# Block means of the first batch's values from single value tiles, two weights laid out contiguously, and a new order of the instructions

## The chip, the cores and the metric

One of the eight cores of a Trainium2 chip runs the kernel. The metric is device microseconds of one execution, as the median of three runs; the trace comes from one more execution, taken by the hardware profiler.

## The reference

Three layers follow each other on 2 batches of 768 tokens of 512 features.

1. Attention of 8 heads of 64. Each query sees a window of 31 keys around it and one summary per block of 32 tokens: the maximum of the block's keys, and the **mean of its values**.
2. Four experts, each a causal attention of width 64 over the 768 tokens. A gate keeps two of them for each token.
3. A channel mix: two blends of each token with the token before it, one through `relu(x @ w_k)**2 @ w_v`, one through `sigmoid(x @ w_r)`, and their product.

```python
k_sum = k.reshape(B, H, nb, block, D).max(axis=3)
v_sum = v.reshape(B, H, nb, block, D).mean(axis=3)
scores_s = scale * np.einsum('bhsd,bhnd->bhsn', q, k_sum) + np.log(block)
a = softmax(np.concatenate([masked(scores_l), scores_s], axis=-1))
x = np.matmul(a, np.concatenate([v, v_sum], axis=2))        # layer 1
...
out = sigmoid(xr @ w_r) * (np.maximum(xk @ w_k, 0.0) ** 2 @ w_v)   # layer 3
```

(The lines are shortened; `softmax` and `masked` stand for the reference's own lines.)

## The kernel before, in words

Layer 1 runs in tiles of 128 tokens, `t` = 0 to 11, six per batch. `stage1_scores` (from L554) makes a tile's scores on TensorE: for `t` below 3 straight from the key tensor `k0` and the key maxima `ksm[0]` (L589, L590), later from copies of its window, the slabs (`slab`, L459, and L584). `stage1_softmax` (L598) adds the mask and takes the maximum on VectorE (L607), takes the exponential on ScalarE (L610), sums and inverts (L613, L615), and scales by the result (L621, or L626 on ScalarE). `stage1_trans` transposes (L650), and `stage1_out` (L655) multiplies with the values (L668). Its operand holds the 96 value rows of a window and 24 rows of block means; `put_val_sums` (L531) copies the means there, on whichever engine the order names (L535 VectorE, L536 ScalarE, L538 GpSimd, L540 a DMA). A tile's result is split into a rounded part and the rest (`rnd`, L368, and `sub`, L376).

The means themselves are products with a constant matrix of 1/32 (`own`, L546): `val_sums` (L496) multiplies a value tile by it, four matmuls of 128 columns each, one per 128 features, into four bands of partitions of one PSUM bank `p`. For the first batch they take the six window tiles of `t` = 0 to 2, which lie two by two in SBUF (`vw`, each 128 rows with some that the next one shares), and one tile of three times 128 rows, `vt0`, loaded by one DMA of 768 KB. `val_sums_out` (L506) then copies the bands to SBUF, 24 x 128 each (L369 on ScalarE, L370 on VectorE). The two weights of the experts that the change touches, `wvg` and `wqk`, are loaded by `load_wvg` (L699) and `load_wqk` (L705), and split into the operands of L761 and L743.

Layer 2 is `proj_all` (L743 queries and keys, L761 values and gates) and `attention` (L843 scores, L903 transposes, L929 values, L971 output). Layer 3 is `rec` (L1123), `hid` (L1174: seven products for eight, with the sums of operands on VectorE or GpSimd at L1036 and L1037, evictions at L1147 and L1192) and `duo` (L1261, the same scheme for the second product). The 64-bit weights of layer 3 are unpacked on VectorE and ScalarE (L1012 to L1022).

The program does not run in the order in which it is written. Each step is recorded as an operation with what it reads and writes, with one or more `ways` (engines), and `Plan.run` (L268) issues them by the table `ORDER`: an entry divided by four is the number of the operation, the rest of the division the way. `HOMES` gives each buffer its slot. All DMAs are issued by SyncE (`load`, L359) in that order. An engine does its own instructions in this order, and waits for others by semaphores.

Of the kernel before, what the change touches and what calls it, by code (L numbers as in the profile page):

```python
# [16 lines left out]
B, H, S, D = 2, 8, 768, 64  # L17
DM = H * D
# [182 lines left out]
)  # L201

CUTS = (5, 9, 12)

EARLY = 3

FIRST = (0,)


class Buf:  # L210

# [104 lines left out]
def attn_moe_rwkv(  # L316
# [39 lines left out]
    def bank(name):  # L356
        return buf(name, [P, 512])
# [1106 lines left out]
```

## Time and profile before

| | us |
|---|---|
| median of three runs | 343.79 |
| lowest and highest of the three | 343.23, 344.01 |
| the profiled execution, its own time | 344.52 |
| its span in the trace | 342.7 |
| TensorE matmuls, busy | 325.3 |
| VectorE busy | 317.9 |
| ScalarE busy | 266.0 |
| GpSimd busy | 102.3 |

The profiled execution's time is 1.82 us more than its span, which is what lies around it, and 0.73 us more than the median of the runs. A busy share is a mean over stages: TensorE is busy in nearly all of the span, and VectorE too, so what an edit is worth is read from the short stretches in which TensorE waits, and from what it waits for there. TensorE's work stands twice in the trace, as weight loads (PEld) and as matmuls (PE); an fp32 matmul of the program shows as two records. The clock granted to TensorE is 1.00 in every stretch but that after the last matmul.

### The profile page before, as it was taken

What the parts mean: (1) busy time and instruction counts of PE and PEld (TensorE: products, weight loads), DVE (VectorE), ACT (ScalarE), POOL (GpSimd) and SP (SyncE); (2) the same over time, 40 slices, a digit from 0 to 9 for tenths busy, and PEclk for the clock granted to TensorE, in tenths of its full rate; (3) what the DMA queues carried; (4) which work ended last, traced back from release to release, by engine and by line L of the source; (5) the groups of instructions that cost most, each with busy time, mean ns of one, the idle gap of its engine ahead of it and who ended that gap; (6) DMA issues with size and microseconds to landing.
All of it is one profiled execution on the core that took longest, in us unless ns stands there. A gap on an engine that the chain in (4) does not pass through costs nothing.

```text
span 342.7 us, 8312 instructions
## 1 busy us (share of the span) xinstructions
PE 325.3 (95%) x3024; PEld 295.0 (86%) x3024; DVE 317.9 (93%) x930; ACT 266.0 (78%) x719; POOL 102.3 (30%) x112
## 2 busy tenths in 40 slices
PE   0899979999999999999999999999999999999995
PEld 0779969988889979789676899999999889999995
DVE  1889988999998898999999999999999999999995
ACT  1699989999898667668688789678996998787630
POOL 0556520514321154141530002125540200414550
PEclk9999999999999999999999999999999999999999
DMA  7999885585061000101142010101004000011223
GB/s 253 348 342 319 281 305 194 166 256 149 2 193 63 2 2 0 63 1 64 61 122 62 9 56 1 61 2 61 2 0 123 3 0 2 0 63 46 80 77 109
DMA packets 20160, 33.80 MB, mean 99 GB/s; under 512 B 2088, under 2 KB 9000, under 8 KB 20120
## 3 DMA queue, kind: packets, MB, share of 16 engines
q1 hardware_dynamic: 20120, 33.28, 29.7%
q8 instruction: 24, 0.39, 0.5%
q14 instruction: 16, 0.13, 0.1%
HBM read 29.63 MB, written 3.15 MB: 96 GB/s over the span
## 4 chain that ended last, share of the span: by engine, by line
PE 82%; DVE 13%; DMA 2%; issue 2%; SPq 1%; ACT 0%; DVEq 0%
PE ps L1261 17%; PE ps L1174 14%; PE ps L743 9%; PE ps L1123 6%; PE ps L761 5%; PE ps L843 5%; PE ps L903 5%; PE ps L929 5%; PE ps L668 4%; PE ps L971 4%; PE ps L650 3%; DVE b L377 3%; DVE t L1100 2%; PE ps L584 2%; DMA ks<-in_kS 2%
## 5 line engine op out<-in xcount | busy, mean ns | idle before, releaser
L1261 PE MATMUL ps<-w,s 128*128 128x256 f32 x336 | 48.9, 281 | 0.0
L1261 PEld LDWEIGHTS ps<-w,s 128*128 128x128 f32 x336 | 43.9, 188 | 0.1
L1174 PE MATMUL ps<-b,w 128*128 128x384 f32 x216 | 41.2, 338 | 0.4 <-DVE b L1192 0.4
L1174 PEld LDWEIGHTS ps<-b,w 128*128 128x128 f32 x216 | 38.1, 188 | 1.0 <-DVE b L1192 0.7
L743 PE MATMUL ps<-b,w 128*128 128x384 f32 x192 | 38.6, 345 | 0.0
L1123 PE MATMUL ps<-w,b 128*128 128x512 f32 x144 | 36.2, 397 | 0.0
L369 ACT ACTIVATE t<-ps 128x384 f32<-128x384 f32 (+1 forms) x59 | 25.9, 468 | 11.2 <-PE ps L903 6.2
L743 PEld LDWEIGHTS ps<-b,w 128*128 128x128 f32 x192 | 32.6, 188 | 0.7 <-issue 0.2
L369 ACT ACTIVATE b<-ps 128x384 f32<-128x384 f32 (+4 forms) x49 | 23.6, 492 | 9.6 <-PE ps L668 2.8
L1123 PEld LDWEIGHTS ps<-w,b 128*128 128x128 f32 x144 | 26.5, 188 | 5.3 <-issue 0.2
L610 ACT ACTIVATE w<-w,nm 128x120 f32<-128x120 f32 x72 | 27.8, 393 | 0.9 <-DVE nm L607 0.7
L369 ACT ACTIVATE b<-t 128x384 fp32r<-128x384 f32 x42 | 20.5, 517 | 6.6 <-DVE t L1100 4.0
L971 PE MATMUL ps<-u,w 128*128 128x384 f32 x96 | 22.0, 352 | 0.6 <-DVE u L377 0.6
L379 POOL TENSOR_TENSOR w<-s,w 128x512 fp32r<-128x512 f32 x13 | 17.8, 1379 | 14.5 <-ACT w L369 12.9
L377 DVE TENSOR_TENSOR b<-t,b 128x384 fp32r<-128x384 f32 x36 | 21.1, 602 | 0.0
L761 PE MATMUL ps<-q,b 128*128 128x260 f32 x144 | 20.9, 291 | 0.0
L1100 DVE SCALAR_TENSOR_TENSOR t<-b,mu,t 128x384 f32<-128x384 f32 x32 | 20.6, 661 | 0.1
L843 PE MATMUL ps<-ks,b 64*128 64x384 f32 (+3 forms) x192 | 20.0, 337 | 0.6 <-DVE t L370 0.6
L929 PE MATMUL ps<-t,b 128*64 128x384 f32 (+2 forms) x144 | 20.6, 421 | 0.0
L1037 POOL TENSOR_TENSOR t<-t,t 128x384 f32<-128x384 f32 (+1 forms) x4 | 5.1, 1286 | 46.8 <-ACT w L369 32.3
L761 PEld LDWEIGHTS ps<-q,b 128*128 128x128 f32 x144 | 18.6, 189 | 0.4 <-issue 0.2
L369 ACT ACTIVATE s<-u 128x512 fp32r<-128x512 f32 x24 | 14.5, 626 | 5.4 <-DVE u L1036 2.3
(204 smaller groups left out, 928.8 us busy)
## 6 DMA issues: line engine op xcount, KB each, us to landing
s<-in_wk SPq DMA_DIRECT2D x8, 512.0 KB
s<-in_wv SPq DMA_DIRECT2D x8, 512.0 KB, 4.1
w<-in_qT SPq DMA_DIRECT2D x12, 256.0 KB, 4.7
out_y<-t SPq DMA_DIRECT2D x24, 128.0 KB, 1.7
w<-in_vp SPq DMA_DIRECT2D x10, 256.0 KB, 4.2
s<-in_wr SPq DMA_DIRECT2D x4, 512.0 KB, 4.6
s<-in_kS SPq DMA_DIRECT2D x6, 320.0 KB
ks<-in_kS SPq DMA_DIRECT2D x4, 400.0 KB
```

Source lines behind the costliest of these rows:

```text
L369: ways = [("act", act(n, sb), lambda: nc.scalar.activation(dst(), src(), AF.Copy)), ("dve", dve2(n) if sb else dve(n), lambda: nc.vector.t ...
L377: ways = [("dve", dve(n), lambda: nc.vector.tensor_tensor(dst(), a(), b().bitcast(F32), ALU.subtract), sb)]
L610: op("act", act(NK, True) + 186, lambda i=i, z=z, pr=pr, nm=nm: nc.scalar.activation(pr()[:, i], pr()[:, i], AF.Exp, bias=nm.t[:, i:i + 1] ...
L743: mm(p.t[:, :C], a[kc].t[:, cols], x.t[:, kc, :], start=(kc == 0 and i == 0), stop=(kc == KC - 1 and i == 2))
L761: mm(p.t[:, :260], x.t[:, kc, tok], a[kc].t, start=(kc == 0 and i == 0), stop=(kc == KC - 1 and i == 2))
L843: mm(ps[e2].t[:, :z - a], q1.t[r, x, tok], ks.t[r, y, a:z], start=n == 0, stop=n == 2)
L929: mm(acc.t[64 * e2:64 * e2 + 64, tq0 * P:(tq0 + cnt) * P], vv.t[:, kb, e * D:(e + 1) * D], th[e2].t[:, i0 * P:(i0 + cnt) * P], start=first ...
L971: mm(p.t[:, :C], a[ep].t[:, m * P:(m + 1) * P], x.t[:, ep, :], start=(ep == 0 and i == 0), stop=(ep == 1 and i == 2))
L1100: op("dve", dve(C) + 60, lambda: nc.vector.scalar_tensor_tensor(tmp(), cur(), mu.t[:, i:i + 1], tmp(), ALU.mult, ALU.add), r=rd, w=[(mb, m ...
L1123: mm(p.t, a.t[:, kc, tok], w[2](), start=(kc == 0 and i == 0), stop=(kc == KC - 1 and i == 2))
L1174: mm(p.t[:, :C], a[2]()[:, o:o + P], x.t[:, u, j], start=not (j or i), stop=j == 1 and i == 2)
L1261: mm(p.t[:, :256], x.t[:, u, j * P:(j + 1) * P], v[2]()[:, col:col + 256], start=not (j or i), stop=j == FC // 2 - 1 and i == 2)
```

## The change

Four things change.

- The means of the first batch use the two window tiles of `t` = 0 alone (`PLAIN = 1`), and five tiles of 128 rows, each in a buffer of its own in the pool `w`, loaded by a DMA of 256 KB. Before they used six window tiles and three tiles in one buffer. So 7 groups of four matmuls are left of 9, and five DMAs stand for one.
- Their results go to two PSUM banks in turn (`p[g % 2]`); ScalarE copies those of one, VectorE those of the other where the order says so.
- `wvg` and `wqk` lie in memory with the rows of a partition together: a partition's 4160 or 4096 bytes are one piece, before four of 1040 or two of 2048.
- `ORDER` and `HOMES` are new throughout. Two planner costs of DMAs (the argument of `load`) changed with them; they have no effect on the program but by the order.

```diff
+PLAIN = 1
...
-        load(tf[0], src, P * S * 4, 360.0 if b else 300.0, w=[(tb, i)])
+        load(tf[0], src, P * (S if b else SPV) * 4, w=[(tb, i)])
...
-                    mm(p.t[32 * g:32 * g + NB, 0:P], own(j, s2), v()[:, g * P:(g + 1) * P],
+                    mm(p[g % 2].t[32 * g:32 * g + NB, 0:P], own(j, s2), v()[:, g * P:(g + 1) * P],
                        start=first and n == 0, stop=last and n == len(tiles) - 1)
...
-                lambda g=g: p.t[32 * g:32 * g + NB, 0:P], P, [p], [(vs, g)])
+                lambda g=g: p[g % 2].t[32 * g:32 * g + NB, 0:P], P, [p[g % 2]], [(vs, g)])
...
-        load(lambda: raw.t, wvg.rearrange("(k p) n -> p k n", p=P), P * 4160, w=[raw])
+        load(lambda: raw.t, wvg, P * 4160, w=[raw])
...
-    vt0 = val_tiles(0, "b6", EARLY, TPB)
+    vt0 = [val_tiles(0, "w", j, j + 1) for j in range(PLAIN, TPB)]
...
-    p = bank("ps")
-    for t in range(EARLY):
+    p = [bank("ps"), bank("ps")]
+    for t in range(PLAIN):
         for s2 in range(2):
             v = vw[t][s2]
             val_sums(v, p, [(t, s2, lambda v=v: v.t)], t + s2 == 0)
-    val_sums(*vt0[:1], p, vt0[1], last=True)
+    for v, tiles in vt0:
+        val_sums(v, p, tiles, last=v is vt0[-1][0])
...
 ORDER = (
-    12, 0, 52, 36, 16, 44, 24, 32, 76, 64, 80, 40, 56, 20, 172, 220, 72, 48, 228, 194, 28, 68, 60, 190, 232, 84,
...
```

Line numbers in the rows of the change are two to four higher than those of the kernel before, for the same code.

**SyncE, the first loads.** `qT` are queries, `kS` keys, `masks` the masks, `vp` values. Before:

```order
L360 DMA w_63<-in_qT 128x512
L360 DMA w_67<-in_qT 128x512
L360 DMA ks_69<-in_kS 128x800 x4
L360 DMA msk_74<-in_masks 128x120
L360 DMA w_76<-in_vp 128x512
```

With the change:

```order
L362 DMA w_65<-in_qT 128x512
L362 DMA ks_67<-in_kS 128x800 x4
L362 DMA msk_72<-in_masks 128x120
L362 DMA w_74<-in_qT 128x512
L362 DMA msk_72<-in_masks 128x240
```

The queries of the second tile (256 KB) stood ahead of the keys and now stand behind them.

**ScalarE, its first instructions**, with the semaphores that they wait for (DMAHW1 to DMAHW4 are the four loads of keys in the change). Before:

```order
L610 ACT_TABLE_LOAD
L610 ACTIVATE b_56_90,sms_65<-b_56_90,nm_91 128x120 [waits DVE_49]
```

With the change:

```order
L371 ACT_TABLE_LOAD [waits DMAHW3_49,DMAHW4_49,DMAHW2_49]
L371 ACTIVATE s_18_120<-ks_67 128x4x160 [waits DMAHW1_49]
L612 ACTIVATE b_60_88,sms_63<-b_60_88,nm_90 128x120 [waits DVE_49]
```

One of the three slab copies of 128 x 640 that GpSimd made now leads ScalarE's order, and the load of the function table stands behind the waits of that copy.

**TensorE around the means** (`ps_290` and `ps_291` are the banks of the means, `b_56`, `b_60` the first tile's weights). Before:

```order
L501 MATMUL ps_290<-w_125,cst_127 24x128 x4
L650 MATMUL ps_303<-cst_127,b_56_90 120x128
L501 MATMUL ps_290<-w_101,cst_127 24x128 x4
L501 MATMUL ps_290<-w_76,cst_127 24x128 x4
L501 MATMUL ps_290<-w_80,cst_127 24x128 x4
L501 MATMUL ps_290<-u_23_132,cst_127 24x128 x4
L650 MATMUL ps_303<-cst_127,b_56_90 120x128 x2
...
L501 MATMUL ps_290<-b_52_196,cst_127 24x128 x12
L650 MATMUL ps_377<-cst_127,b_67_151 120x128 x3
```

With the change:

```order
L503 MATMUL ps_290<-w_127,cst_125 24x128
L503 MATMUL ps_291<-w_127,cst_125 24x128
L652 MATMUL ps_318<-cst_125,b_60_88 120x128 x3
L652 MATMUL ps_327<-cst_125,b_60_88 120x128
...
L503 MATMUL ps_290<-w_201,cst_125 24x128
L503 MATMUL ps_291<-w_201,cst_125 24x128
L652 MATMUL ps_327<-cst_125,b_60_88 120x128
L652 MATMUL ps_364<-cst_125,b_72_154 120x128
```

Before, 4 matmuls of the means stood ahead of the first transpose, and 7 transposes and 16 matmuls of scores between the last of the means and the first use of them (L668). Now 12 of 28 stand ahead of the first transpose, and 10 transposes and 32 matmuls of scores between the last and the first use.

## Rows read from the trace of the kernel before

**Rows 1.** The page: span, and busy time by engine (us, share, instructions).

```profile
span 342.7 us, 8312 instructions
PE 325.3 (95%) x3024; PEld 295.0 (86%) x3024; DVE 317.9 (93%) x930; ACT 266.0 (78%) x719; POOL 102.3 (30%) x112
```

**Rows 2.** Stretch 10 to 20 us: length; busy PE, PEld, DVE, ACT, POOL; PEclk; DMA; GB/s.

```profile
10.00:20.00 10.00, 8.79 (x266) 7.22 (x262) 8.67 (x63) 8.49 (x45) 6.62 (x11) 1.00 1.01 353
```

**Rows 3.** Chain that ended last, in order of time: start us, us, what.

```profile
3.06 6.96 DMA ks<-in_kS
...
20.02 0.83 PE ps L501 x24
...
216.12 44.46 PE ps L1174 x252
...
279.36 59.69 PE ps L1261 x504
```

**Rows 4.** Timeline of SyncE's queue: start us, us, what is issued.

```profile
0.72 0.87 SPq L360 DMA_DIRECT2D w<-in_qT  x2
```

**Rows 5.** Timeline of ScalarE: start us, us, instruction [idle before it, releaser].

```profile
0.72 1.28 ACT L610 ACT_TABLE_LOAD   x1 [0.72 <-PEq L1453]
11.22 0.39 ACT L610 ACTIVATE b<-b,nm 128x120 f32<-128x120 f32 x1 [9.22 <-DVE nm L607]
...
20.87 1.11 ACT L369 ACTIVATE w<-ps 24x128 f32<-24x128 f32 x4 [0.33 <-PE ps L501]
```

**Rows 6.** Groups by form: line engine op shapes, count, busy us, mean ns, idle before.

```profile
L372 POOL TENSOR_SCALAR s<-ks 128x640 f32<-128x640 f32 x3 | 2.1, 727 | 9.3 <-DMA ks<-in_kS 9.3
L369 ACT ACTIVATE w<-s 128x512 fp32r<-128x512 f32 x19 | 11.8, 622 | 0.1
```

**Rows 7.** Timelines of GpSimd and of TensorE, first weights and first transpose.

```profile
15.02 1.93 POOL L621 TENSOR_TENSOR b<-b,rss 128x480 f32<-128x480 f32 x2 [1.77 <-DVE rss L615]
...
17.17 0.33 PE L650 MATMUL ps<-cst,b 128*120 128x128 f32 x1
```

**Rows 8.** Timelines of VectorE and of TensorE, the first use of the means.

```profile
22.02 1.17 DVE L535 COPY w<-w 24x512 f32<-24x512 f32 x2 [1.19 <-ACT w L369]
...
23.24 2.11 PE L668 MATMUL ps<-b,w 120*64 120x64 f32 x64 [0.54 <-DVE w L535]
```

**Rows 9.** What TensorE waited for: total us, times, longest us.

```profile
PE ps L668 <- issue: 1.8, 1, 1.8
PE ps L584 <- issue: 1.1, 1, 1.1
...
PE ps L1174 <- DVE b L1192: 0.4, 1, 0.4
```

**Rows 10.** Groups by form of VectorE, and four of a kind in its timeline.

```profile
L370 DVE COPY w<-ps 120x512 f32<-120x512 f32 x7 | 4.8, 685 | 0.1
L370 DVE COPY t<-ps 128x384 f32<-128x384 f32 x17 | 9.2, 548 | 1.6 <-PE ps L884 0.9 <-PE ps L903 0.5
L1100 DVE SCALAR_TENSOR_TENSOR t<-b,mu,t 128x384 f32<-128x384 f32 x32 | 20.6, 661 | 0.1
L377 DVE TENSOR_TENSOR w<-s,w 128x512 fp32r<-128x512 f32 x14 | 10.4, 740 | 0.0
...
204.18 1.96 DVE L377 TENSOR_TENSOR b<-t,b 128x384 fp32r<-128x384 f32 x4
```

**Rows 11.** Timelines of VectorE and GpSimd where both read SBUF.

```profile
212.05 1.39 DVE L1100 SCALAR_TENSOR_TENSOR t<-b,mu,t 128x384 f32<-128x384 f32 x1
...
211.81 1.21 POOL L1037 TENSOR_TENSOR t<-t,t 128x384 f32<-128x384 f32 x1 [32.29 <-ACT w L369]
...
314.31 7.45 POOL L379 TENSOR_TENSOR s<-u,s 128x512 fp32r<-128x512 f32 x1 [0.26 <-POOL t L1037]
```

**Rows 12.** DMA issues: out<-in, count, KB each, median us to landing.

```profile
w<-in_vp SPq DMA_DIRECT2D x10, 256.0 KB, 4.2
...
s<-in_wqk SPq DMA_DIRECT2D x2, 512.0 KB, 10.1
```

More of the change, by code (lines that the diff above doesn't have):

```diff
@@ L500, in go @@
                 for g in range(4):
-                    mm(p.t[32 * g:32 * g + NB, 0:P], own(j, s2), v()[:, g * P:(g + 1) * P],
+                    mm(p[g % 2].t[32 * g:32 * g + NB, 0:P], own(j, s2), v()[:, g * P:(g + 1) * P],
                        start=first and n == 0, stop=last and n == len(tiles) - 1)
-        op("pe", 230 * len(tiles), go, r=[vt, cst], w=[p], stream="p1v", mode="quarter")
+        op("pe", 230 * len(tiles), go, r=[vt, cst], w=p[:1] if p[0] is p[1] else p, stream="p1v", mode="quarter")
     def val_sums_out(b, p):
@@ L523, in sums1 @@
             key_sums(1, i, t, [lambda t=t: t.t] * 2, kS[1, :, i, HALO:HALO + S])
-        p = bank("ps")
+        p = [bank("ps")] * 2
         for j in range(0, TPB, 2):
@@ L707, in load_wqk @@
             raw = buf("s4", [P, 2, 512])
-            load(lambda raw=raw: raw.t, wqk[256 * k2:256 * k2 + 256].rearrange("(k p) n -> p k n", p=P), P * 4096,
+            load(lambda raw=raw: raw.t, wqk[:, 2 * k2:2 * k2 + 2], P * 4096,
                  w=[raw])
@@ L1353, in attn_moe_rwkv @@
     stage1(0, 1)
-    p = bank("ps")
-    for t in range(EARLY):
+    p = [bank("ps"), bank("ps")]
+    for t in range(PLAIN):
         for s2 in range(2):
@@ L1410, in _layout @@
     wk = moe_wk.reshape(2, 2, DM, D).transpose(2, 0, 1, 3).reshape(DM, 2, 1, P)
-    d["wqk"] = np.concatenate([wq, wk], axis=2).reshape(DM, 512)
-    d["wvg"] = np.concatenate([moe_wv.transpose(1, 0, 2).reshape(DM, E * D), moe_w_gate], axis=1)
+    d["wqk"] = np.concatenate([wq, wk], axis=2).reshape(KC, P, 512).transpose(1, 0, 2)
+    wvg = np.concatenate([moe_wv.transpose(1, 0, 2).reshape(DM, E * D), moe_w_gate], axis=1)
+    d["wvg"] = wvg.reshape(KC, P, E * D + E).transpose(1, 0, 2)
     d["wo"] = moe_wo.reshape(2, P, DM).transpose(1, 0, 2)
```

287 rows, old and new, of tables (HOMES, ORDER) are left out of this document.

## The prediction

> **What bounds the kernel now.** I read the busy shares first, then the chain that ended last, then what TensorE waited for, and last the timelines of the first 25 us. The shares [rows 1] show TensorE busy for 325.3 of 342.7 us and VectorE for 317.9: there is little idle time to win, 17.4 us on TensorE, and most of it lies ahead of the first keys and behind the last matmul. The chain [rows 3] says what holds each stretch. It begins with the loads of the keys, the last of which lands at 3.06 + 6.96 = 10.02 us. It then stays on TensorE nearly without a break, leaves it for VectorE for some thirty microseconds ahead of 216 us, and from 216.12 us on is TensorE up to the last few instructions: 252 records of L1174, and at last 504 of L1261, each without a wait. So the kernel is bound by TensorE behind a start that DMA sets, and a microsecond that is won early on TensorE is kept if VectorE, which has hardly more room, comes earlier too. TensorE's waits [rows 9] are few: 1.8 and 1.1 us for which the profile names no releaser ("issue"), and 0.4 us for VectorE at L1174; to these comes the wait of 0.54 us at 23.24 [rows 8], for the block means. These waits, the start, and the work itself are all that the change can shorten.
>
> **The change, part by part.**
>
> *The keys come earlier.* The queries of the second tile leave their place ahead of the keys. SyncE's queue spends 0.87 us on issuing two loads of queries [rows 4], so the keys are issued some 0.43 us earlier; and 262 kB less pass ahead of the last of them, at the 353 GB/s of the first full stretch [rows 2] 0.74 us. The bounds are 0.4 and 0.75 us, and I take 0.6: the transfers, not the issue, fill these microseconds, but the queue of the value loads behind the keys competes too.
>
> *ScalarE starts with a copy.* In the trace the function table is loaded at 0.72 us in 1.28 us, while nothing else could run, and the first exponential starts at 11.22 us [rows 5]. Now the table load waits for the keys, at about 10.02 - 0.6 = 9.4 us, and the slab copy follows. The copy of 128 x 640 was on GpSimd, 0.73 us; ScalarE takes 0.62 us for 128 x 512 [rows 6], by size 0.78 us for 640 columns. So ScalarE is free at 9.4 + 1.28 + 0.78 = 11.5 us, 0.25 us later than its first exponential before. The first tile's weights were scaled by GpSimd from 15.02 to 16.95 us, and the first transpose stood at 17.17 [rows 7]; both move 0.25 us late, to 17.2 and 17.4. TensorE, 0.6 us early, does not idle for that, since 8 more matmuls of the means now stand ahead of the first transpose: 16 records at 0.83 / 24 = 0.035 us [rows 3] are 0.55 us, and it arrives at 17.17 - 0.6 + 0.55 = 17.1. The 0.6 us are therefore spent on work that stood later; 0.1 to 0.3 us of waiting may be left, which lies within the bounds above. What covers ScalarE's late start is this reordering; without it 0.6 us would be lost again.
>
> *Fewer matmuls for the means.* 36 become 28, 8 fewer, or 16 records at 0.035 us: **0.55 us** less on TensorE, in a stretch where it is the chain.
>
> *The wait for the means.* Before, the last of them ended at 20.85 us, ScalarE copied four bands in 1.11 us [rows 5], VectorE copied the result behind it from 22.02 us, having waited 1.19 us, and TensorE started L668 at 23.24 us after a wait of 0.54 us [rows 8]. With two banks two engines copy two bands each, some 0.55 us in place of 1.11; and three transposes and 16 matmuls of scores more stand in between on TensorE. The wait of 23.24 - 20.85 = 2.4 us is then covered: **0.54 us** less, 0 at worst. VectorE's idle 1.19 us goes too, and so it keeps pace. Late next is the value weight `wvg`, whose parts are the operands of L761.
>
> *The loads.* Five loads of 256 KB replace one of 768 KB. A load of 256 KB lands 4.2 us after its issue [rows 12]. Up to the last value tile SyncE now issues some 0.5 MB less, since four window tiles move behind it, so none of the means waits for its tile. The `wqk` loads stand behind 0.26 MB more than before, 0.75 us at 353 GB/s; they landed 10.1 us after issue [rows 12], in a full queue, and their first user came later still. The contiguous weights move the same bytes in fewer pieces; the price of a piece stands in no row, and as no transfer but the keys is on the chain, I take 0 for it, between a loss of 0.75 us and a gain of as much.
>
> *The rest of the order.* Counted in the two orders, VectorE has 676 instructions ahead of its first L1192 in place of 682. What goes is above all four evictions of 120 x 512 (4 x 0.69), five of 128 x 384 (5 x 0.55) and two scalings of 128 x 480 (some 0.7 each, by size); what comes is three subtractions of 128 x 512 (3 x 0.74), three evictions of 24 x 128 and smaller ones (some 1.7 together). At these means of forms [rows 10] the difference is 6.9 - 3.9 = 3.0 us. Neighbours overlap: four L377 of 128 x 384 took 1.96 us, 0.49 apiece, where the mean of 128 x 512 gives 0.56 by size; so nearer 2.6 us. TensorE's wait there is only 0.4 us [rows 9], so I book **0.4 us** and leave the rest as room. The two waits without a releaser I leave where they are: the trace shows no cause, and the new order has the same instructions around the first.
>
> *GpSimd gets more.* It has 129 rows where it had 117. For that the trace has a warning: at 212.05 us one L1100 of VectorE took 1.39 us beside a GpSimd instruction that began at 211.81 [rows 11], where the mean of its form is 0.66 [rows 10]. Twelve more such pairs would be 12 x 0.73 = 8.8 us of VectorE; none costs nothing. I take 0, since VectorE's own work has become less, and since GpSimd was used as densely beside it before. The Trainium skill's page "SBUF — State Buffer", section "Who interferes with whom", says that a GpSimd instruction that reads SBUF and a VectorE instruction with two SBUF inputs share a port that one of them holds for its whole length, so that the other fully blocks. By that rule every added pair is at risk, and a sum with half of them would end 4.4 us higher than mine.
>
> The sum is 0.6 + 0.55 + 0.54 + 0.4 = 2.1 us. Against the profiled execution's own 344.52 us (span 342.7 and 1.82 around it) that gives 342.4; that execution lies 0.73 above the median of 343.79, so the median becomes **341.7 us**.
>
> **The rivals.**
>
> *Slower: GpSimd is starved in the last stage.* In `duo`, GpSimd had two instructions of 128 x 512 and now has five, sums that VectorE made before, and ScalarE and VectorE wait for their results in order. At 314.31 us such a subtraction took 7.45 us [rows 11], where VectorE never paused. The same page's rule agrees with that row. Each of the three new ones can be some 6 us late. TensorE stalls if its next operand is later than its lead; if half of the 6 us is covered, one such stall costs 3.0 us and gives 341.7 + 3.0 = 344.7. For it speaks that the chain of this stage is 504 records of TensorE without a break [rows 3], so that any wait is a loss; against it that the long one at 314.31 cost TensorE nothing. It decides as soon as one operand is late by more than the 2.1 us that were won.
>
> *No change.* The early microseconds are won, but the new order opens a wait elsewhere, or the unexplained waits [rows 9] come once more: 1.5 us, between 1.1 and 1.8, gives 343.2, and with the start's gain lost to ScalarE 343.8. For it speaks that VectorE is as full as TensorE, so that an order must hold both.
>
> *Much faster.* VectorE's 2.6 us less work closes the waits in the middle as well, and the start brings its full 0.75: some 2 us more, 339.7. Against it: TensorE's own work shrinks by 0.55 us alone, so this needs nearly every wait gone.
>
> **How the numbers follow.** The forecast has a chance of 0.50, much faster 0.14, no change 0.13, slower 0.23. A measurement tells 0.2% from no change, 0.7 us. The first two are faster by more than that: 0.64; no change is 0.13; slower 0.23. The range goes from 339.3, below the much faster case, to 345.0, just above the slower one, and leaves out half of that case, with two stalls or more, and a few in 100 below.
>
> **What would show it.** The chain's first DMA should end near 9.4 us, ScalarE's table load should stand behind it, and its first exponential near 11.5. TensorE should go from the means to L668 without a wait, and begin L761 some 1.5 to 2 us earlier than before. The last stage should again be all TensorE. The prediction is wrong if TensorE waits in `duo` behind a GpSimd instruction of several microseconds, if its matmuls begin no earlier than before at 50 us, or if waits without a releaser grow.

## The result: slower, and where the time went

The changed kernel takes **346.45 us** (median of five runs, 345.92 to 346.59), the kernel before 344.01 us beside it. The ratio is 1.0067, with a 95% interval of 1.0049 to 1.0085: 2.4 us slower, where 2.1 us faster was forecast, and outside of the range. The profiled executions are 346.08 and 344.52 us; their spans 343.9 and 342.7. So the two traced executions lie 1.6 us apart, 1.1 of it in the span.

The page of the changed kernel, span and busy time by engine (answers to [rows 1]):

```profile
span 343.9 us, 8297 instructions
PE 328.0 (95%) x3008; PEld 295.8 (86%) x3008; DVE 318.6 (93%) x927; ACT 264.5 (77%) x713; POOL 100.1 (29%) x124
```

TensorE has 16 records fewer, as counted, and yet 2.7 us more busy time (its ends are modelled, so short waits are in it); VectorE has 3 instructions fewer and 0.7 us more. Work shrank and time grew. The chain that ended last (start us, us, what; answers to [rows 3]) shows where:

```profile
2.59 6.04 DMA ks<-in_kS
...
21.90 0.56 issue
...
23.09 1.08 PE ps L670 x32
...
26.27 1.27 PE ps L763 x9
...
201.70 11.79 PE ps L1176 x66
213.51 0.56 DVE ks L1194
...
245.80 3.10 DVE t L1102 x3
...
288.92 51.17 PE ps L1263 x430
```

The last keys land earlier than forecast, at 2.59 + 6.04 = 8.63 us in place of 10.02. Less of that is left on TensorE: L670 begins without a wait, but TensorE stands 0.56 us in the scores just ahead of it (at 21.90 us), and L763 begins 1.1 us earlier than L761 did, where 1.5 to 2 us were forecast. The kernel before, in its chain:

```profile
27.35 1.08 PE ps L761 x9
```

But the changed kernel's chain leaves TensorE at 213 us, and from there to 289 us it runs over VectorE, with two stretches of some 5 us on ScalarE, where before it was TensorE from 216 us to the end. What TensorE waited for (total us, times, longest; answers to [rows 9]):

```profile
PE ps L591 <- DMA ks<-in_kS: 4.7, 1, 4.7
PE ps L586 <- issue: 2.3, 2, 1.7
PE ps L592 <- DVE ksm L489: 1.4, 4, 0.4
PE ps L1176 <- ACT b L371: 1.2, 1, 1.2
PE ps L1263 <- DVE s L379: 0.6, 1, 0.6
PE ps L1176 <- DVE b L379: 0.5, 1, 0.5
PE ps L1176 <- DVE b L1194: 0.5, 1, 0.5
PE ps L670 <- issue: 0.3, 1, 0.3
```

The first three belong to the start. The 1.8 us ahead of L668 have become 0.3; but they differ from execution to execution, since the trace of `contig` (below), with the order of the kernel before, has 0.2 us there. In place of the 0.4 us at L1174 there are three waits in the same stage and one in the next. How much lead there was to lose is read from the records of this one product in three stretches. The kernel before (stretch, length, busy PE with its records, PEld, PEclk, DMA, GB/s, for L1174 alone):

```profile
190.00:210.00 20.00, 7.71 (x41) 7.33 (x42) 1.00 0.08 28
210.00:250.00 40.00, 39.58 (x226) 39.26 (x225) 1.00 0.08 27
```

The changed kernel, L1176 alone:

```profile
190.00:210.00 20.00, 10.89 (x61) 10.80 (x62) 1.00 0.08 28
210.00:250.00 40.00, 37.67 (x207) 35.75 (x206) 1.00 0.08 27
```

At 210 us it is 20 records ahead; at 44.46 / 252 = 0.176 us each [rows 3] that is **3.5 us**, more than the 2.1 that were forecast. It is a true lead: behind 210 us both kernels have the same matmuls left but for these 20 records, 871 before and 851 now. Some 1.2 us of it is the traced execution of the kernel before, whose 871 records are left at 210.12 us, and in the trace of `contig` at 208.89. In the next 40 us the changed kernel does 19 records less, and the lead is gone. Its first L1263 begins at 279.01 us, 0.2 us ahead of the kernel before, and the last matmul ends at 340.07 us, 1.03 us behind it, so another 1.2 us go in duo.

What VectorE did there is seen in two timelines of the changed kernel (start us, us, instruction). VectorE, from 216 us:

```profile
216.04 1.95 DVE L1102 SCALAR_TENSOR_TENSOR t<-b,mu,t 128x384 f32<-128x384 f32 x2
218.03 1.27 DVE L1038 TENSOR_TENSOR t<-t,t 128x384 f32<-128x384 f32 x1
219.22 1.23 DVE L1016 TENSOR_SCALAR s<-s 128x512 f32<-128x512 f32 x1
220.37 0.55 DVE L1194 TENSOR_TENSOR b<-ps,ks 128x384 f32<-128x384 f32 x1
220.84 0.54 DVE L1149 TENSOR_TENSOR ks<-ps,ks 128x384 f32<-128x384 f32 x1
221.30 1.14 DVE L1038 TENSOR_TENSOR b<-b,b 128x384 f32<-128x384 f32 x1
```

GpSimd, at the same time:

```profile
216.56 1.02 POOL L1039 TENSOR_TENSOR b<-b,b 128x384 f32<-128x384 f32 x1 [1.85 <-ACT b L371]
217.66 1.22 POOL L1039 TENSOR_TENSOR b<-b,ks 128x384 f32<-128x384 f32 x1
218.83 2.51 POOL L1039 TENSOR_TENSOR t<-t,t 128x384 f32<-128x384 f32 x2
221.29 0.74 POOL L1039 TENSOR_TENSOR s<-s 128x256 f32<-128x256 f32 x1
```

Four of VectorE's instructions, the second L1102, the L1016 and the L1038 at 218.03 and 221.30, take 1.1 to 1.4 us in place of 0.4 to 0.6, each beside a GpSimd instruction; the L1016 is the clearest, three times as long. The L1194 and L1149 beside the second half of 218.83's pair keep their 0.55 us: they read PSUM (`ps`) and one operand from SBUF. In the kernel before the same stage had as many GpSimd instructions, 15. VectorE in it:

```profile
228.30 1.47 DVE L1147 TENSOR_TENSOR ks<-ps,ks 128x384 f32<-128x384 f32 x3
...
232.84 0.55 DVE L1036 TENSOR_TENSOR t<-t,t 128x384 f32<-128x384 f32 x1
```

and GpSimd beside it:

```profile
228.53 1.03 POOL L379 TENSOR_TENSOR b<-t,b 128x384 fp32r<-128x384 f32 x1 [3.51 <-ACT b L369]
232.46 1.80 POOL L1037 TENSOR_TENSOR t<-t,t 128x384 f32<-128x384 f32 x1 [2.90 <-DVE b L377]
```

At 228.53 GpSimd ran beside three evictions from PSUM, and neither was slower. At 232.46 it began while VectorE worked from SBUF, and there GpSimd took 1.80 us and VectorE kept its time. Adding up, for each VectorE instruction, what it took above the median of its form, where that is over 0.25 us: from 210 to 290 us VectorE lost **4.7 us** before, in 7 instructions, and **7.9 us** now, in 11 (other ways of grouping give up to 5.1 and 8.1; the expectations below have 4.7 or 4.9, and 8.1). All of the 4.7 us lie in hid; of the 7.9 us 6.8 do, and 1.1 at 287 us in duo. In both traces every such instruction, 22 and 28 in the whole span, has a GpSimd instruction beside it. The Trainium skill's page "SBUF — State Buffer", section "Who interferes with whom", tells it so: a VectorE instruction with two SBUF inputs and a GpSimd instruction that reads SBUF want the same port, the one that starts first holds it, and a VectorE instruction with at most one SBUF input does not contend, outside of its two-port modes. The trace agrees, with the rows above (the L1016 is taken up at the end).

The longest wait shows how this reaches TensorE. In VectorE's timeline three L1102 take 3.18 us where three took some 1.6:

```profile
245.72 3.18 DVE L1102 SCALAR_TENSOR_TENSOR t<-b,mu,t 128x384 f32<-128x384 f32 x3
```

GpSimd works at that time:

```profile
246.10 1.38 POOL L1039 TENSOR_TENSOR u<-ks 128x512 f32<-128x512 f32 x1 [2.71 <-ACT ks L1187]
247.43 1.06 POOL L381 TENSOR_TENSOR q<-s,q 128x256 fp32r<-128x256 f32 x1
```

ScalarE's next eviction stands behind them and waits 2.47 us:

```profile
249.00 0.49 ACT L371 ACTIVATE b<-ps 128x384 f32<-128x384 f32 x1 [2.47 <-DVE t L1102]
```

and TensorE 1.20 us for that:

```profile
249.54 1.32 PE L1176 MATMUL ps<-b,w 128*128 128x384 f32 x6 [1.20 <-ACT b L371]
```

### The profile page after: what moved, and what is told of

The parts are those of the page before. It is cut to its first block, busy times and chain, and to the rows that moved or that the text cites. A ratio compares the mean times of both kernels' runs of the same rounds, so it can differ in the third digit from the quotient of the medians.

```text
span 343.9 us, 8297 instructions
## 1 busy us (share of the span) xinstructions
PE 328.0 (95%) x3008; PEld 295.8 (86%) x3008; DVE 318.6 (93%) x927; ACT 264.5 (77%) x713; POOL 100.1 (29%) x124
## 4 chain that ended last, share of the span: by engine, by line
PE 70%; DVE 21%; ACT 3%; issue 3%; DMA 2%; SPq 0%; DVEq 0%; ACTq 0%
PE ps L1263 15%; PE ps L745 9%; PE ps L905 5%; PE ps L763 5%; PE ps L931 5%; PE ps L973 5%; PE ps L1125 5%; PE ps L845 5%; PE ps L1176 4%; PE ps L670 3%; PE ps L652 3%; PE ps L586 2%; DVE b L379 2%; DVE b L1149 2%; DVE t L1102 2%
## 5 line engine op out<-in xcount | busy, mean ns | idle before, releaser
L1263 PE MATMUL ps<-w,s 128*128 128x256 f32 x336 | 49.2, 281 | 0.7 <-DVE s L379 0.6
L1263 PEld LDWEIGHTS ps<-w,s 128*128 128x128 f32 x336 | 44.0, 188 | 1.2 <-DVE s L379 1.1
L1176 PE MATMUL ps<-b,w 128*128 128x384 f32 x216 | 41.6, 340 | 2.3 <-ACT b L371 1.2
L1176 PEld LDWEIGHTS ps<-b,w 128*128 128x128 f32 x216 | 37.7, 188 | 4.3 <-ACT b L371 1.5
L745 PE MATMUL ps<-b,w 128*128 128x384 f32 x192 | 39.1, 345 | 0.0
L371 ACT ACTIVATE t<-ps 128x384 f32<-128x384 f32 (+1 forms) x62 | 26.9, 470 | 11.5 <-PE ps L905 6.5
L371 ACT ACTIVATE b<-ps 128x384 f32<-128x384 f32 (+4 forms) x53 | 25.4, 496 | 5.7 <-DVE t L1102 2.5
L371 ACT ACTIVATE b<-t 128x384 fp32r<-128x384 f32 x39 | 19.6, 522 | 5.1 <-DVE t L1102 2.5
L1102 DVE SCALAR_TENSOR_TENSOR t<-b,mu,t 128x384 f32<-128x384 f32 x32 | 21.3, 684 | 1.2 <-ACT t L390 1.1
L763 PE MATMUL ps<-q,b 128*128 128x260 f32 x144 | 22.0, 293 | 0.0
L379 DVE TENSOR_TENSOR b<-t,b 128x384 fp32r<-128x384 f32 x39 | 21.9, 576 | 0.0
L381 POOL TENSOR_TENSOR w<-s,w 128x512 fp32r<-128x512 f32 x11 | 14.7, 1337 | 21.9 <-ACT w L371 10.7
L973 PE MATMUL ps<-u,w 128*128 128x384 f32 x96 | 21.0, 347 | 0.0
L381 POOL TENSOR_TENSOR b<-t,b 128x384 fp32r<-128x384 f32 x5 | 5.1, 1021 | 54.3 <-ACT b L371 54.2
L763 PEld LDWEIGHTS ps<-q,b 128*128 128x128 f32 x144 | 18.7, 188 | 0.8 <-issue 0.4
```

The source lines that it names most:

```text
L371: ways = [("act", act(n, sb), lambda: nc.scalar.activation(dst(), src(), AF.Copy)), ("dve", dve2(n) if sb else dve(n), lambda: nc.vector.t ...
L379: ways = [("dve", dve(n), lambda: nc.vector.tensor_tensor(dst(), a(), b().bitcast(F32), ALU.subtract), sb)]
L745: mm(p.t[:, :C], a[kc].t[:, cols], x.t[:, kc, :], start=(kc == 0 and i == 0), stop=(kc == KC - 1 and i == 2))
L763: mm(p.t[:, :260], x.t[:, kc, tok], a[kc].t, start=(kc == 0 and i == 0), stop=(kc == KC - 1 and i == 2))
L973: mm(p.t[:, :C], a[ep].t[:, m * P:(m + 1) * P], x.t[:, ep, :], start=(ep == 0 and i == 0), stop=(ep == 1 and i == 2))
L1102: op("dve", dve(C) + 60, lambda: nc.vector.scalar_tensor_tensor(tmp(), cur(), mu.t[:, i:i + 1], tmp(), ALU.mult, ALU.add), r=rd, w=[(mb, m ...
```

## The experiments

Two theories. Theory 1: VectorE, which has no room in hid, is slowed there beside GpSimd, and that takes the lead away. Theory 2: it is the order itself, its waits or the amount of work left to VectorE. Each kernel was timed beside the kernel before, at 344.07 to 344.18 us.

**Old last part on the new start.**

```diff
-ORDER = (changed kernel, 2156 steps)
+ORDER = (changed kernel, its first 1560 steps) + (kernel before, the 596 steps that are left, with their engines)
```

> The changed kernel up to its 1560th step of 2156 (about 205 us), and the remaining 596 steps in the order and on the engines that the kernel before had; buffers of that part moved to free slots. Theory 1 (VectorE beside GpSimd in layer 3): the changed kernel's TensorE stood 3.6 us ahead at the eighth part of its L1176, and lost that and 0.8 us more up to L1263, because VectorE lost 8.1 us from 210 to 290 us beside GpSimd instructions, where it had lost 4.7. With the old last part the lead is kept: 344.0 - 3.6 = 340.4 us, between 340 and 342. Theory 2 (the lead is worth nothing, as VectorE's remaining work sets the end whatever the order): 344 to 346.4 us, no better than either kernel.

Measured: 344.72 us, ratio 0.999 (0.9953 to 1.0028). Theory 1 in this form fell: the lead was lost again, and at once, and the time lies in the range of theory 2. TensorE waited 2.2 us for L1194, perhaps since the old part expects other work of VectorE to be done when it begins. With a new wait at the seam the run does not part the two theories. Six of the ten runs, the profiled one among them, had a mean granted clock of 0.995 and took 344.7 to 345.8 us, the four at 1.00 took 342.9 to 343.5. What happened to the clock is in the windows of this kernel (length; busy PE, PEld, DVE, ACT, POOL; PEclk; DMA; GB/s):

```profile
212.00:216.00 4.00, 2.61 (x10) 2.62 (x11) 3.86 (x9) 2.13 (x5) 0.00 (x0) 0.77 0.08 9
216.00:220.00 4.00, 4.00 (x20) 4.00 (x20) 2.57 (x5) 0.87 (x2) 0.45 (x1) 0.80 0.33 122
220.00:224.00 4.00, 4.00 (x25) 4.00 (x24) 3.87 (x6) 2.97 (x7) 2.11 (x2) 1.00 0.00 0
...
215.00:216.00 1.00, 1.00 (x5) 1.00 (x4) 0.86 (x2) 0.00 (x0) 0.00 (x0) 0.50 0.31 37
216.00:217.00 1.00, 1.00 (x4) 1.00 (x4) 0.02 (x1) 0.00 (x0) 0.00 (x0) 0.50 0.76 254
```

After the wait TensorE was granted less than the full 2.4 GHz: from 215 to 217 us the clock was 0.50, its level of 1.2 GHz. In the 4 us from 216 it did 20 records where the next 4 us have 25. In this execution the wait cost more than its length.

**New last part on the old start.**

```diff
-ORDER = (kernel before, 2152 steps)
+ORDER = (kernel before, its first 1560 steps) + (changed kernel, the 592 steps that are left, with their engines)
```

> The mirror: the kernel before up to its 1560th step of 2152, and the rest in the order and on the engines of the changed kernel. Theory 1: the last part alone costs 3.6 + 0.8 = 4.4 us less what room it has, so 346 to 348.5 us. Theory 2: 344 us as before, within 1 us.

Measured: 349.99 us, ratio 1.0157 (1.0081 to 1.0233). This is on the side of theory 1, and past its range (346 to 348.5). In the trace the last part takes longer: from 871 records left to the end of the last matmul it is 134.3 us, where the kernel before takes 128.9. But the traced execution, the slowest of the four at 352.45 us, also comes to that point 2.5 us later, and TensorE waits 2.1 us for L1192: a part that was made for another start meets other buffers and waits. So the run points at the last part, and its size is not to be trusted.

**The layout alone.**

```diff
-        load(lambda: raw.t, wvg.rearrange("(k p) n -> p k n", p=P), P * 4160, w=[raw])
+        load(lambda: raw.t, wvg, P * 4160, w=[raw])
```

(and `wqk` in the same way)

> The kernel before with nothing but the two weights laid out contiguously per partition. Theory 1 and 2 alike: 0 within 0.5 us (343.5 to 344.5 us), since no weight load is on the chain. A rival that the layout itself slows or speeds the first loads: a difference of 0.75 us or more either way.

Measured: 343.95 us, ratio 0.9991 (0.9956 to 1.0026). The layout makes no difference that shows, as was taken; the interval leaves room for 1.5 us less to 0.9 us more.

**The means alone, two attempts.** In the first the new loads came in a bad place.

> The kernel before in its own order and on its own engines, with only the means changed: two window tiles and five value tiles, two banks, the four more loads right behind the first. By the prediction's terms 0.55 us less matmuls, and some of the wait of 0.54 us: 343 us if VectorE lets TensorE keep it, 344 if not. If the edit of the means, and not the order, were what slows the changed kernel: 346 us.

Measured: 347.01 us, ratio 1.0074 (1.0041 to 1.0106). TensorE waited 3.2 us for queries (`w<-in_qT`), whose load was issued only at 9.94 us, behind value loads. It tells nothing of the means, but what a load in a wrong place costs. The second put them right; the rows are those of SyncE's queue behind the constants (window and value tiles are all `in_vp`):

```diff
-L360 DMA cst_127<-in_consts 128x280
-L360 DMA u_23_132<-in_vp 128x512
-L360 DMA u_24_189<-in_vp 128x512
-L360 DMA b_52_196<-in_vp 128x3x512
+L363 DMA cst_127<-in_consts 128x280
+L363 DMA w_132<-in_vp 128x512
+L363 DMA w_189<-in_vp 128x512
+L363 DMA w_196<-in_vp 128x512
+L363 DMA w_198<-in_vp 128x512
+L363 DMA w_200<-in_vp 128x512
+L363 DMA u_23_202<-in_vp 128x512
+L363 DMA u_24_204<-in_vp 128x512
```

> The kernel before in its own order and on its own engines, with the means and the contiguous weights of the changed kernel: the first four value tiles are loaded where the four window tiles stood, and these with the fifth where the load of 768 KB stood. (In the run before this one the loads of queries and values were interchanged, and the keys' scores waited 3.2 us for queries.) By the prediction's terms 0.55 us of matmuls less and up to 0.54 us of wait less: 343 us if TensorE's gain is kept to the end, 344 if VectorE from 184 to 216 us takes it. If the edit of the means slows the kernel: above 345.

Measured: 343.08 us, ratio 0.9977 (0.9962 to 0.9991). The edit of the means is worth 1.0 us by the medians (0.3 to 1.3 by the interval). Its two terms, 0.55 and 0.54, add up to that, but the trace bears out only the first. L671 begins without a wait, and TensorE stands as long just ahead of it, in L587:

```profile
22.06 1.05 PE L587 MATMUL ps<-s,w 64*64 64x120 f32 x32 [0.48 <-issue]
23.22 0.98 PE L671 MATMUL ps<-b,w 120*64 120x64 f32 x26
```

The first L764 begins at 27.06 us, 0.47 us earlier than L761 in `contig`, whose first wait without a releaser is as long as here (1.65 us): near the 0.55 us of the matmuls. The gain is kept to the end, 0.7 us at the last matmul against that trace.

**The queries behind the keys, alone.**

```diff
 L360 DMA w_63<-in_qT 128x512
-L360 DMA w_67<-in_qT 128x512
 L360 DMA ks_67<-in_kS 128x800 x4
 L360 DMA msk_72<-in_masks 128x120
+L360 DMA w_74<-in_qT 128x512
```

> The kernel before with one load moved: the queries of the second tile, from ahead of the keys to behind them. The prediction's first term alone: the last keys land 0.6 us earlier (the changed kernel shows 1.4), TensorE ends the first scores as much earlier. If the gain is kept: 343.0 to 343.4 us; if VectorE's chain from 184 to 216 us takes it: 344.0.

Measured: 343.34 us, ratio 0.9988 (0.9969 to 1.0006), 0.7 us less by the medians; the interval still holds no change. The first L761 begins at 26.40 us in place of 27.11. TensorE's 27 records of L584 that end the first scores begin at 13.21 us in its chain, against 14.58 before.

**GpSimd's sums in hid cut to one column.** This leaves out most of 11 sums.

```diff
+def one(ap):
+    return ap[:, 0:1] if TRIMMING[0] else ap
...
-                     ("pool", pool_tt(n), lambda: nc.gpsimd.tensor_tensor(dst(), a(), b(), fn))], r=r, w=w)
+                     ("pool", pool_tt(n), lambda: nc.gpsimd.tensor_tensor(one(dst()), one(a()), one(b()), fn))], r=r, w=w)
```

> The changed kernel, where 11 of the 15 GpSimd instructions that it has in hid (sums of L1039 that write over one of their operands, 213 to 266 us) work on 1 column in place of 256 or 384: the rest of these sums is left out. Nothing else is moved. Theory 1 (VectorE is slowed beside GpSimd): 0.89 + 0.72 + 0.82 + 0.68 + 0.55 + 0.55 + 0.44 = 4.65 us of VectorE's slow instructions lie beside these 11, so VectorE gets up to 4.65 us back, and TensorE keeps its lead of 3.6 us: 342.5 to 344 us, where the changed kernel took 346.45. Theory 2 (the order of the last part stalls TensorE through its dependences, or VectorE simply has too much left): 346 to 346.5 us.

Measured: 343.1 us, ratio 0.9968 (0.9947 to 0.999): 3.35 us less than the changed kernel, with every step in its place. This decides for theory 1: the same order, the same semaphores and the same amount of work for VectorE, and the loss is gone with GpSimd's reading and writing. A rival is that GpSimd's own results came too late, which the cut mends as well: ScalarE waited 1.3 us for one of them in the changed kernel, and waits 0.5 us here. But the three waits of TensorE that are gone (0.6, 0.5 and 0.5 us) were for VectorE, and none of its waits there was for GpSimd. From 210 to 290 us TensorE makes 457 records. The windows of 210 to 290 us, this kernel (columns as above):

```profile
210.00:290.00 80.00, 78.67 (x457) 74.30 (x455) 76.29 (x148) 66.77 (x141) 10.02 (x16) 1.00 0.08 27
```

and the changed kernel:

```profile
210.00:290.00 80.00, 76.97 (x432) 71.39 (x431) 77.79 (x144) 65.02 (x138) 18.56 (x16) 1.00 0.08 27
```

VectorE makes 148 instructions in 76.29 us there, and 144 in 77.79 with GpSimd's whole sums beside it. The wait of 1.2 us for `ACT b` stays, and fits: the two GpSimd instructions at 246.10 and 247.43, beside which its L1102 are slow, were not among the 11; VectorE still loses 3.5 us beside GpSimd in this stretch.

**All of hid's GpSimd work on VectorE**, in the changed kernel. Of the 15 rows that leave GpSimd, the first three:

```diff
-L381 TENSOR_TENSOR b_737_3423<-t_3351,b_737_3423 128x384
-L1039 TENSOR_TENSOR t_3351<-t_3438,t_3351 128x384
-L1039 TENSOR_TENSOR b_680_3451<-b_680_3451,b_681_3526 128x384
...
```

> The changed kernel with all 15 GpSimd instructions of hid on VectorE, at the same place of the order. VectorE gets 8.1 - 1.1 = 7.0 us back that it lost beside them up to 266 us, and has 12 x 0.47 + 3 x 0.6 = 7.4 us more to do. Theory 1: 346.45 + 0.4, within 345.5 to 347.5 us. Theory 2 (VectorE has too much to do, and GpSimd takes work off it): 346.45 + 7.4 less the half microsecond of waits, 351 us or more.

Measured: 344.4 us, ratio 1.001 (0.9995 to 1.0025). With 15 instructions more for VectorE the kernel is 2 us faster than with GpSimd's help. Theory 2 would have 351 us or more. Theory 1's range was missed too, on the other side: its own figure was 2.4 us too high. It had weighed VectorE's sums alone, and not that TensorE's wait of 1.2 us for `ACT b` goes with the slow L1102, and the one of 0.5 us for L1194; 0.4 us lie outside of the span (below). The kernel **with one sum of duo more on VectorE**:

```diff
-L1039 TENSOR_TENSOR u_905_4355<-b_725_3730 128x512
```

> The changed kernel with all 15 GpSimd instructions of hid on VectorE (344.4 us alone), and in addition the first GpSimd sum of duo (128 x 512, at 286.64 us, beside which an L379 of VectorE took 1.78 us in place of 0.67). Theory 1: 1.1 us of VectorE's time is saved and 0.6 added, 344.4 - 0.5 = 343.9 us. Theory 2 (more work for VectorE is what costs): 345 us.

Measured: 343.49 us, ratio 0.9984 (0.9965 to 1.0004). Against the 344.4 us of the kernel with 15 it is 0.9 us less, where 0.5 was expected; the two intervals overlap, so by the times alone it is not shown. The traces agree with it: the last 504 records of TensorE take 60.31 us here and 60.99 with the 15.

**The same edit in the kernel before**, whose 15 are others:

```diff
-L1037 TENSOR_TENSOR t_3310<-t_3398,t_3310 128x384
-L379 TENSOR_TENSOR b_732_3390<-t_3357,b_732_3390 128x384
...
```

> The kernel before with its 15 GpSimd instructions of hid (211 to 268 us) on VectorE, in the old order: the same edit that brought the changed kernel from 346.45 to 344.4 us. Theory 1 (what counts is what VectorE reads while GpSimd works): VectorE lost only 4.9 us beside these 15, and would have 15 x 0.5 = 7.5 us more to do: 2 us or more slower where TensorE had no wait, 346 to 347 us. A rival (GpSimd in hid is a loss in any order): 342 to 343.5 us.

Measured: 345.69 us, ratio 1.0039 (1.0018 to 1.0061): 1.5 us slower. So GpSimd in hid is no loss in itself: in the old order it saves 1.5 us, in the new one it costs 2. What makes the old order's instructions cheaper is not shown by a run. That they fall more often beside evictions from PSUM explains little: of the time in which GpSimd and VectorE work at once from 210 to 270 us, some 31% lies beside VectorE instructions that read PSUM before, and some 26% now. The traces show who waited: GpSimd's instructions of 128 x 384 in hid took 1.31 us in the mean before and 1.11 now, so in the old order it was rather GpSimd that was late.

**The old choice of engines in the new order**, from the 1480th step on. GpSimd's rows:

```diff
+L1039 TENSOR_TENSOR t_3385<-t_3426,t_3385 128x384
 L381 TENSOR_TENSOR b_737_3423<-t_3351,b_737_3423 128x384
-L1039 TENSOR_TENSOR t_3351<-t_3438,t_3351 128x384
-L1039 TENSOR_TENSOR b_680_3451<-b_680_3451,b_681_3526 128x384
+L1017 TENSOR_SCALAR s_811_3408<-s_811_3408 128x512
...
```

> The changed kernel in its own order, with the engines of the kernel before for every step from the 1480th on (19 steps from VectorE to GpSimd, 19 back, 6 between VectorE and ScalarE). If the choice of the sums for GpSimd is what slows VectorE: 343 to 344.5 us. If it is which of VectorE's instructions happens to run beside them, an engine choice made for another order does not help: 345.5 to 347.5 us.

Measured: 343.94 us, ratio 0.9986 (0.9969 to 1.0003), 2.5 us less than the changed kernel. The new order as such is then no slower than the old; most of the loss goes with the choice of engines. VectorE's loss beside GpSimd from 210 to 290 us, added up as above, is 4.0 us in it.

**The two early edits together, in the old order** (both diffs stand above):

> The kernel before in its own order, with the two early edits together: the means (with the contiguous weights) and the queries of the second tile behind the keys. Alone they gave 343.08 and 343.34 us beside 344.07. If they add up, as both only bring TensorE forward and its chain had no wait after 216 us: 344.07 - 0.99 - 0.73 = 342.35 us, better than both kernels. If VectorE's chain from 184 to 216 us lets only one of them pass: 343 us.

Measured: **342.22 us** (341.33 to 342.91), ratio 0.993 (0.9909 to 0.9951). They add up, and this kernel is faster than both. Its chain (start us, us, what) ends as that of the kernel before, 1.7 us earlier (its traced execution, 342.91 us, is the slowest of its six, and that of the kernel before has the wait of 1.8 us):

```profile
277.68 59.81 PE ps L1264 x504
```

## Why the prediction was wrong, point by point

- **The step that failed** is "GpSimd gets more": "I take 0, since VectorE's own work has become less, and since GpSimd was used as densely beside it before". The count, 129 rows for 117, was the wrong measure. In hid GpSimd has 15 instructions in both orders; what changed is beside which of VectorE's instructions they run. The price was 7.9 - 4.7 = 3.2 us of VectorE from 210 to 290 us, with a wait of ScalarE and TensorE behind it. With GpSimd's sums cut 3.35 us come back, with the old engines 2.5. The kernel with the two early edits alone is 4.2 us faster than the changed one, so 0.9 to 1.7 us of what the rest of the order costs stay open. The 4.4 us that the prediction itself set beside its sum would have made the forecast 2.3 us slower, and it was 2.4; that is luck in the size, since they price six more pairs, and hid has no GpSimd instruction more.
- **What was booked for "the rest of the order"** was 0.4 us. The order brought more: VectorE's first L1194 starts at 208.4 us, where the first L1192 started at 215.5, and TensorE led by 3.5 us at 210 (2.3 against the trace of `contig`). It was given back by 279 us.
- **The keys**: booked 0.6 us, measured 10.02 - 8.63 = 1.4 at the landing; by itself the edit is worth 0.7 us at the end. The sign and the reason were right, and the 0.6 us near what is left at the end.
- **ScalarE's late table load** shows no cost. It stood at 8.72 us, the copy behind it, and the first exponential started at 10.65 us, not at 11.5 (answers to [rows 5]):

```profile
8.72 1.28 ACT L371 ACT_TABLE_LOAD   x1 [8.72 <-DMA ks<-in_kS]
10.01 0.74 ACT L371 ACTIVATE s<-ks 128x640 f32<-128x640 f32 x1
10.65 0.38 ACT L612 ACTIVATE b<-b,nm 128x120 f32<-128x120 f32 x1
```

- **The means**: 0.55 and 0.54 us booked, 1.0 us measured with that edit alone (0.3 to 1.3). The matmuls are right. The wait is not: with the edit TensorE stands 0.48 us ahead of L587, and 0.56 us ahead of L586 in the changed kernel, where it stood 0.54 us ahead of L668. In the kernel with both early edits the profile names ScalarE's copy of the means (`ACT w L372`) as what ended this wait, of 0.49 us. The traces put the gain at 0.5 to 0.7 us, so that the medians agree with the whole sum is in part luck.
- **The layout**: 0 booked, 0.1 us measured, within the interval. The loads have no run of their own.
- **The rivals**: the one on the slower side had GpSimd held up by VectorE, in duo. In duo GpSimd's longest instruction took 3.76 us, and TensorE's one wait there is 0.6 us, for VectorE. It was VectorE that was held up by GpSimd, mostly one stage earlier, in hid. That "a microsecond that is won early on TensorE is kept if VectorE, which has hardly more room, comes earlier too" was right: it held for the two early edits, and VectorE's time was what the new order lost. The "no change" rival named VectorE as full as TensorE, so that what it lost had no room to vanish in.

The interval on `q1_behind` alone still holds no change, and the waits that the profile calls "issue" ahead of L586 (1.7 us here, 1.1 before) were not settled; `contig`, with the order of the kernel before, has 1.65 us there, so they differ between executions of one order.

## What to carry to other kernels

Price an instruction that goes to GpSimd by what VectorE does beside it: next to evictions from PSUM it was free here, next to a VectorE instruction that works from SBUF one of the two was late, VectorE by up to 1.1 us. Where two engines are both full, look stage by stage which has a lead, and whether the stage behind it can take it; a lead of 3.5 us was lost in 70 us. And try the parts of a change one by one in the old order before the whole order is made anew: two small edits gave 2.0 us, the whole change cost 2.4.

## What was not expected of the hardware

- VectorE's L1016, which has only one SBUF input, was slowed as well: 1.23 us in place of 0.41 beside GpSimd at 219.22. The same page of the Trainium skill says that instructions of this kind can take the shared port in their faster modes; the row fits that, though it does not show the mode.
- After a wait of 2.2 us TensorE's granted clock was 0.77 and 0.80 in two stretches of 4 us (above): a mean, with 0.50, its level of 1.2 GHz, from 215 to 217 us. In the changed kernel TensorE stood for 1.70 us at 14.38, and the granted clock stayed at 1.00.
- The time outside of the span is 2.2 us in the changed kernel, 2.2 to 2.3 in the one with cut sums, 2.1 to 2.2 in the one with the old engines, and 1.7 to 1.9 in the others. The changed kernel with hid's GpSimd work on VectorE has 1.8. So 0.4 of the 2.4 us lie outside of all that the trace shows; why was not found.
